# Scores in three parts, the last columns in two, and a new written-out order, in a sparse-attention and feed-forward kernel

## The chip, the cores and the metric

The kernel runs on one core of a Trainium2 chip. The metric is the device time of one execution in microseconds (us), the median over runs. Names of engines as the profile has them: PE is TensorE (matmuls; PEld is its weight load), ACT is ScalarE, DVE is VectorE, POOL is GpSimd and SP is SyncE. PEq, SPq, POOLq and ACTq are their instruction queues.

## What is computed

Sparse attention over 4 batches, 8 heads, 768 positions of 64 numbers: each query sees the keys less than 16 positions away, and one summary key (an elementwise maximum) and one mean value for each block of 32 positions. Its output, as 3072 rows of 512, goes through a feed-forward layer with a hard swish between two matrix products.

```python
k_sum = k.reshape(B, H, nb, block, D).max(axis=3)          # block = 32
v_sum = v.reshape(B, H, nb, block, D).mean(axis=3)
scores_l = scale * q @ k.T      # kept where |i - j| < 16
scores_s = scale * q @ k_sum.T + log(block)
a = softmax(concat(scores_l masked, scores_s))
x = a @ concat(v, v_sum)        # as [3072, 512]
h = x @ w_in                    # w_in [512, 2048]
g = h * clip(h + 3, 0, 6) / 6
out = g @ w_out                 # w_out [2048, 512]
```

## The kernel before

**Attention.** Queries go in tiles of 64 (12 a batch), each with a window of 96 keys and the 24 block keys, so 120 keys; a scores matmul gives keys down the partitions and queries along the columns. `kaug` holds windows and block maxima, `qT` the queries, `vaug` values with a column of ones (for the softmax sum) and the spread block sums, `at` the exponentials. Heads come in pairs p = 0 to 3. A batch is done in two halves of 384 queries; half 0 is tiles 6 to 11, half 1 tiles 0 to 5. Each half is one tile s of the feed-forward part (s = 0 to 7, 384 rows).

**Feed-forward.** `f1(s, ft)` (L656) makes 128 of the 2048 hidden columns: four matmuls of 384 columns, a relu on ACT (L670), and a gate on DVE (L671) that reads the same PSUM bank and the relu's result. For s = 0 and ft below 5 the four matmuls are operations of their own. `f2(s, ts, part)` (L674) sums 16 matmuls of 512 columns in four parts, then a copy to `ot` and a store by SP. For s = 7, ts = 1 the columns are done as two halves; the second half is copied as two quarters, one by ACT, which also issues its DMA (`finish`, L698), and one by DVE (L702), which SP stores (L703).

**PSUM.** Eight banks: three `h`, one `o`, and two `S` tiles of two banks. **The order.** Every operation is named: a letter, a place and a number (`s120.0` is the first operation of the scores of batch 1, heads u = 2, half 0). `ORDER` (L29) lists the names by hand as one sequence for all engines; `:A` or `:D` says which of ACT and DVE does an operation that either can do (`EITHER`). `Plan.issue` (L133) goes down the list, gives each buffer the slot of its pool that came free longest ago, and issues. Each engine then runs its own operations first in, first out, and waits by semaphores for what they read or overwrite; two engines' accesses to one PSUM tile are kept in list order as well. Tokens that begin with `~`, `-`, `_` or `=` are filler matmuls (`keep`, L778): n of 512, n of 128, n of 64 columns, or one of n x 64.

Letters: `c` constants (c.5 block indicator, c.6 and c.7 ones columns of `vaug`, c.8 to c.15 empty rows of `vaug`); `K Q V I O H` loads by POOL (`I` is w_in, `O` is w_out); `k` (L383) k transposes of batch 0, .1 block maxima, .2 and .3 copies of the halves, .4 the maxima's spread; `q` q transposes and copies (L410, L428); `h` copies of the neighbouring 32 rows of v (L357); `w` (L448) batches 1 to 3: transposes of k and q by DVE, neighbour rows, maxima, spread; `s` scores (L475, L501), with exponential on ACT and mask on DVE; `u` block sums of v and their copies (L526, L546); `v` values (L566, L609): matmuls, reciprocal and scale on DVE (L595), then for s below 4 a transpose on PE and a copy, else block transposes on DVE (L642) and four SP moves of four DMAs (L646); `F` and `G` are `f1` and `f2`. v03.5 is the last copy of batch 0's first half.

In `scores4` (L501) the scores of batches 1 to 3 are done for two head pairs u and one half: 48 matmuls of 64 columns into two `S` tiles, then for each tile an exponential of 120 x 768 (L520) and a mask of 96 x 768 (L521).

## Time and profile before

| | us |
|---|---|
| median of 3 runs | 217.43 |
| runs | 217.16 to 218.7 |
| span of the profiled execution | 215.4 |
| TensorE busy in it | 207.6 |
| VectorE busy in it | 162.1 |
| ScalarE busy in it | 136.0 |

The profiled execution has no time of its own beside its span (first to last instruction); the runs are timed from outside, some 2 us more. In the profile, a group's row has the line, engine, operation, output and inputs with shapes, the count, busy time and mean duration in ns, then the idle time of the engine ahead of them and what ended it. A row of the timeline has start, length, engine, line, what it does, how often, and in brackets the idle time ahead. A row by stage has the stretch, its length, then busy time and instructions of PE, PEld, DVE, ACT and POOL, the granted TensorE clock (1.00 is full), and the DMA engines' share and rate.

### The profile page before, as it was taken

How to read it: one execution, taken by the hardware profiler on the slowest of the kernel's cores; microseconds unless marked ns; L12 is line 12 of the kernel's file. 1: busy time of each engine (PE TensorE's matmuls, PEld its weight loads, DVE VectorE, ACT ScalarE, POOL GpSimd, SP SyncE). 2: the span in 40 equal slices, each digit the busy share in tenths (PEclk: the TensorE clock that was granted, in tenths of full speed). 3: DMA queues.
4: the chain of work that ended last, by engine and by line, in shares of the span. 5: the costliest groups of instructions: out<-in, count | busy, mean ns of one | idle time of the engine just before them, and what ended most of it. 6: DMA issues, size and time to landing. Idle time of an engine off the chain costs nothing.

```text
span 215.4 us, 6065 instructions
## 1 busy us (share of the span) xinstructions
PE 207.6 (96%) x2521; PEld 119.9 (56%) x2548; DVE 162.1 (75%) x318; ACT 136.0 (63%) x264; POOL 49.7 (23%) x66
## 2 busy tenths in 40 slices
...
DMA packets 91724, 22.68 MB, mean 105 GB/s; under 512 B 82224, under 2 KB 88752, under 8 KB 91696
## 3 DMA queue, kind: packets, MB, share of 16 engines
...
q8 instruction: 20, 0.33, 0.6%
q10 hardware_dynamic: 144, 0.07, 0.1%
q14 instruction: 8, 0.07, 0.1%
...
## 4 chain that ended last, share of the span: by engine, by line
PE 82%; SPq 5%; DMA 4%; issue 2%; DVE 2%; POOL 2%; ACT 1%; ACTq 0%; POOLq 0%
PE h L666 36%; PE o L683 29%; PE h L683 5%; SPq L648 4%; DMA first<-in_q_dram 3%; PE S L623 3%; PE S L512 2%; DMA out_dram<-ot 1%; ACT vaug L241 1%; POOL first L305 1%; PE S L636 1%; PE S L666 1%; PE h L581 1%; PE S L489 1%; PE S L553 1%
## 5 line engine op out<-in xcount | busy, mean ns | idle before, releaser
L666 PE MATMUL h<-x,win 128*128 128x384 bf16 x500 | 91.1, 326 | 0.1
L670 ACT ACTIVATE r<-h 128x384 f32<-128x384 f32 x125 | 58.7, 492 | 38.8 <-PE h L666 36.8
L671 DVE SCALAR_TENSOR_TENSOR g<-r,h 128x384 bf16<-128x384 f32 x125 | 65.9, 546 | 22.6 <-ACT r L670 20.0
L683 PE MATMUL o<-wout,g 128*128 128x512 bf16 x309 | 78.0, 379 | 1.9 <-issue 0.8
L666 PEld LDWEIGHTS <-win 128*128 128x128 bf16 x512 | 48.7, 98 | 35.5
L683 PEld LDWEIGHTS <-g 128*128 128x128 bf16 x400 | 38.4, 98 | 37.6 <-issue 0.3
L520 ACT ACTIVATE at<-S 120x768 bf16<-120x768 f32 x24 | 18.6, 810 | 5.5 <-PE S L512 5.4
L241 ACT COPY ot<-o 128x512 f32<-128x512 f32 x17 | 10.0, 587 | 15.4 <-PE o L683 14.2
L521 DVE TENSOR_TENSOR at<-at,mask 96x768 bf16<-96x768 bf16 x24 | 12.6, 549 | 2.0 <-ACT at L520 1.6
L605 DVE TENSOR_TENSOR xn<-S,rc 128x768 bf16<-128x768 f32 x14 | 13.3, 950 | 0.3
L343 POOL DMA_DIRECT2D vaug<-in_v_dram x10 | 11.9, 1194 | 0.4 <-DMA first<-in_k_dram 0.2
L241 DVE COPY ot<-h 128x512 f32<-128x512 f32 x2 | 1.3, 686 | 13.7 <-PE h L683 13.7
L683 PE MATMUL h<-wout,g 128*128 128x256 bf16 (+1 forms) x64 | 11.4, 326 | 0.0
L467 DVE TENSOR_REDUCE red<-kaug 128x24 bf16<-128x768 bf16 x12 | 11.2, 943 | 0.1
L241 ACT COPY vaug<-vaug 32x640 bf16<-32x640 bf16 (+3 forms) x17 | 8.9, 574 | 0.6 <-DMA vaug<-in_v_dram 0.3
L241 ACT COPY vaug<-vs 24x1536 bf16<-24x1536 bf16 x6 | 8.8, 1468 | 0.6 <-DVE vs L241 0.5
L782 PE MATMUL o<-idle 128*128 128x64 bf16 (+2 forms) x70 | 7.5, 287 | 1.1 <-DVE idle L287 1.1
L455 DVE STREAM_TRANSPOSE kaug<-kraw 128x768 bf16<-128x768 bf16 x8 | 8.1, 1025 | 0.3 <-PE S L512 0.3
L623 PEld LDWEIGHTS <-at 120*64 120x64 bf16 x336 | 6.3, 111 | 3.0 <-issue 1.6
L333 POOL DMA_DIRECT2D kraw<-in_k_dram x8 | 5.9, 740 | 8.5 <-DVE kaug L455 7.4
L642 DVE STREAM_TRANSPOSE y<-xn 128x768 bf16<-128x768 bf16 x8 | 7.6, 965 | 0.2
L512 PEld LDWEIGHTS <-kaug 32*128 32x128 bf16 x576 | 5.3, 92 | 4.4 <-issue 3.6
...
## 6 DMA issues: line engine op xcount, KB each, us to landing
out_dram<-ot SPq DMA_DIRECT2D x19, 256.0 KB, 2.3
vaug<-in_v_dram POOLq DMA_DIRECT2D x6, 384.0 KB, 12.9
...
win<-in_moe_w_in_dram POOLq DMA_DIRECT2D x3, 512.0 KB, 10.0
...
x<-y SPq DMA_DIRECT2D x64, 24.0 KB, 2.0
first<-in_k_dram POOLq DMA_DIRECT2D x6, 192.0 KB, 12.3
first<-in_q_dram POOLq DMA_DIRECT2D x6, 192.0 KB, 12.3
```

Source lines behind the costliest of these rows:

```text
L241: {"ACT": nc.scalar.copy, "DVE": nc.vector.tensor_copy, "POOL": nc.gpsimd.tensor_copy}[eng](o, i)
L343: op("POOL", "dma128", lambda: nc.gpsimd.dma_start(out=o[BLK:WIN, a:z, 0:D], in_=rows[:, a:z]), w=[("v", b % 2, c) for c in range(lo, hi)] ...
L467: op("DVE", "max", lambda: nc.vector.tensor_reduce(red.slot[:], w[:, :, BLK:WIN].rearrange("p t (n c) -> p t n c", n=2), axis=AX.X, op=ALU ...
L512: nc.tensor.matmul(X[g // 2].slot[:, g % 2, i * QB:(i + 1) * QB], kaug[2 * u + m][rows, t], qT[rows, 2 * u + m, t * QB:(t + 1) * QB], star ...
L520: op("ACT", "exp", lambda a=a, e=e: nc.scalar.activation(a, X[e].slot[0:KEYS, :, 0:HALF], AF.Exp, scale=scl), r=[X[e]], w=[("at", p, half)])
L521: op("DVE", "masking", lambda m=m: nc.vector.tensor_tensor(m, m, mask[:, low(half):low(half) + HQ].unsqueeze(1).to_broadcast([WIN, 2, HQ, ...
L605: nc.vector.tensor_tensor(o, src[..., 0:D], r.unsqueeze(len(r.shape)).to_broadcast(list(o.shape)), op=ALU.mult)
L623: nc.tensor.matmul(X.slot[64 * c:64 * c + 64, i, m:m + D + 1], a[:, t * QB:(t + 1) * QB], vaug[b % 2][0:KEYS, h, t, 0:D + 1], start=True, ...
L666: nc.tensor.matmul(bank(h)[:, 0:HALF], w_in_sb[:, kt, cols], xt[s].slot[:, kt], start=(kt == 0), stop=(kt == NP - 1))
L670: op("ACT", "relu", lambda: nc.scalar.activation(r.slot[:], bank(h)[:, 0:HALF], AF.Relu, bias=0.5, scale=1.0 / 6.0), r=[h], w=[r])
L671: op("DVE", "gate", lambda: nc.vector.scalar_tensor_tensor(gt[s].slot[:, ft], r.slot[:], 1.0, bank(h)[:, 0:HALF], op0=ALU.min, op1=ALU.mul ...
L683: nc.tensor.matmul(o.slot[:, a:z], gt[s].slot[:, ft, ts * 128:(ts + 1) * 128], w_out_sb[:, ft, a:z], start=(ft == 0), stop=(ft == NFT - 1))
```

## The change

Four things. `scores4` works in three parts of a batch in place of four: parts 0 and 1 are a pair u with tiles 4 to 11, part 2 is both pairs with tiles 0 to 3; each part is 64 matmuls, two exponentials of 120 x 1024, and masks (two of 96 x 1024, or four of 96 x 512). `at` becomes one tensor for that. The last tile's second half of columns becomes two groups of 16 matmuls of 128 columns: 384 to 512 ends as other tiles do (a copy, an SP store), 256 to 384 ends with ACT's copy and DMA. `ORDER` is rewritten from beginning to end, with other engines for some copies; it has no place where ACT and DVE read one PSUM tile next to each other. And the copy of q's first 16 columns has a key of its own (`qa`), for which only part 2 waits.

```diff
@@ -27,62 +27,62 @@
 ORDER = """
-c.0 K00.0 c.7 c.17 c.6 c.8:A K01.0 c.10:D c.5 c.1 _40 -15 k0.0 k0.2:A c.18 ~1 =2 k1.0 K02.0 ~12 =3 k2.0 k3.0 c.15:D c.2 c.3
-s000.0 k0.3:A c.13:D c.4 c.11:A k1.1 Q00.0 q0.0 k1.4 k0.1 c.20 k1.2:A Q01.0 ~2 =5 q1.0 k0.4 k1.3:D c.9:A c.14:A c.19 k2.3:A
-q0.1:A s000.1 q0.2:A =1 s010.0 s010.1 k2.2:A k3.2:D k3.3:D k3.1 V00.0 h000.0:D h001.0:D k2.1 k2.4 s000.2 ~2 =5 v00.0 V01.0 u0.0
-h010.0:D s020.0 c.16 s010.2 q1.2:A u0.3:D u0.1:D u0.4:D v01.0 v01.1 v01.2 v00.1 q1.1:A V02.0 h020.0:A h021.0:A h011.0:A v00.2
-s020.1 v01.3 v00.3 V03.0 u1.0 u1.3:A h030.0:D s030.0 k3.4 ~2 s030.1 u1.4:D v01.4 h031.0:D Q0w0.0 Q0w1.0 v01.5:D Q0w2.0 =1 q3.0
-q3.1:D q2.0 u1.1:A u1.2:D s020.2 v02.0 v02.1 v02.2 s021.0 v02.3 s030.2 v03.0 v03.1 q2.1:A v03.2 s011.0 v03.3 v00.4 v00.5:D v02.4
-s021.1 s011.1 s021.2 v03.4 v03.5:D s011.2 v02.5:A s031.0 s031.1 s001.0 s031.2 I2.0 F0x3.0 F0x3.1 F0x3.2 F0x3.3 F0x3.4 F0x3.5
-I4.0 F0x6.0 F0x6.1 F0x6.2 F0x4.0 F0x4.1 F0x4.2 F0x4.3 v411.0 v411.1 F0x5.0 F0x4.4 F0x4.5 v411.2 s001.1 I8.0 u0.2:A s001.2 F0x8.0
...
-G71x0.0 G62x0.4:D G62x0.5 F7x7.2 F7x11.0 F7x11.1 G61x0.0 F7x11.2 F7x14.0 G71x0.1 G71x0.2 G71x256.0 G61x0.1 F7x14.1 F7x14.2
-G71x0.3 G71x0.4:A G72x0.0 G72x0.1 G71x0.5 G41x0.5 G70x0.0 G61x0.2 G61x0.3 G61x0.4:A G52x0.5 G70x0.1 G70x0.2 G72x0.2 G50x0.0
-G50x0.1 G61x0.5 G50x0.2 G50x0.3 G72x0.3 G70x0.3 G50x0.4:A G50x0.5 G70x0.4:D G70x0.5 G60x0.0 G60x0.1 G60x0.2 G72x0.4:D G72x0.5
-G60x0.3 G71x256.1 G71x256.2 G60x0.4:D G60x0.5 G71x256.3 G71x256.4 G71x256.5 G71x256.6
+c.0 K00.0 K01.0 c.1 K02.0 _40 -14 k0.0 c.2 Q00.0 Q01.0 c.18 c.19 c.17 c.3 k0.1 =3 s010.0 =7 k1.0 k1.3:D c.16 s000.0 ~8 =6 k2.0
+c.6 k0.3:A k0.2:A k1.2:A k3.0 c.8:A V00.0 V01.0 c.20 c.4 k1.1 c.9:A k2.1 k3.3:A ~4 q0.0 k3.2:A c.5 k0.4 k2.4 k1.4 q0.1:A ~2 =3
+s000.1 k3.1 q0.2:A s000.2 =4 s010.1 s010.2 q1.0 V02.0 V03.0 h000.0:D q1.1:D k2.2:A =3 v00.0 s030.0 =7 s020.0 Q0w0.0 Q0w1.0
+k2.3:A u0.0 u0.1:A Q0w2.0 k3.4 q1.2:D c.10:D s030.1 s020.1 h010.0:D v01.0 u0.3:D I2.0 I4.0 h011.0:D I8.0 I0.0 I12.0 v01.1 v00.1
+s020.2 c.11:A s030.2 v01.2 h020.0:D v01.3 v00.2 v00.3 ~1 =6 v02.0 =6 v01.4 u0.2:D u1.0 u1.1:A v00.4 v01.5:D h030.0:D v00.5:A
+u1.3:A =5 v02.1 v03.0 v03.1 q3.0 v02.2 v02.3 v03.2 u0.4:D h001.0:A h031.0:A q3.1:D K13.0 q2.0 v02.4 v02.5:A =6 s031.0 q2.1:D
+v03.3 u1.2:D s031.1 K10.0 K12.0 F0x2.0 F0x3.0 F0x2.1 s001.0 v03.4 K11.0 Q1w1.0 s031.2 v03.5:D u1.4:D s001.1 s001.2 s011.0
+F0x3.1 F0x3.2 F0x2.2 F0x2.3 s011.1 s011.2 F0x3.3 s021.0 F0x3.4 F0x3.5 F0x2.4 s021.1 Q1w4.0 F0x5.0 F0x2.5 Q1w2.0 v410.0 v410.1
+F0x6.0 h021.0:A F0x7.0 F0x6.1 s021.2 v410.2 v411.0 F0x7.1 v410.3 v410.4:A F0x6.2 F0x7.2 v411.1 v411.2 F0x9.0 F0x9.1 F0x9.2
...
+V10.0 Q20.0 Q23.0 w12.0 w12.2 w12.3:D w12.1:D G02x0.3 G02x0.4:A K22.0 K21.0 Q22.0 K23.0 K20.0 V22.0 w13.3:D F1x12.2 c.15:D
+F1x4.2 s11.0 G00x0.0 G00x0.1 G00x0.2 G00x0.3 s11.1 s11.2 s10.4 c.13:D u4.0 h120.0:A s11.3 s11.4 h130.0:A G00x0.4:A h100.0:D
+h110.0:D s10.2 u4.1:A u4.4:A u4.3:D G01x0.0 u4.2:D h111.0:A G01x0.1 H2.0 v100.0 u4.5:D v101.0 v100.1 v101.1 v100.2 v101.2
...
+F4x13.2 w31.1 w30.2:A F4x6.1 w31.4:A F4x6.2 w32.1 F4x9.2 G32x0.3 w33.1 w32.2:A w33.3 F4x11.0 G22x0.5 v211.4 w33.4:D G32x0.4:A
+F4x11.1 u6.5:D F4x11.2 F4x7.0 v211.6 s30.0 F4x12.0 G30x0.0 G30x0.1 w32.5:A w32.4:A w31.5:D s30.3 s30.1 F4x7.1 F4x12.1 s31.0
...
+F4x3.0 F4x12.2 F4x3.1 G30x0.2 G30x0.3 s31.1 s31.3 v211.5 G20x0.5 F5x11.0 s30.4 F4x3.2 s30.2 F4x7.2 s31.4 G30x0.4:A F4x1.0
+F5x11.1 F5x7.0 F5x7.1 F4x1.1 w33.5:A s31.2 G32x0.5 F5x11.2 F5x7.2 w30.5:A v301.0 v300.0 v301.1 F4x1.2 v301.2 F4x5.0 F5x4.0
...
+G51x0.5 G71x0.2 F7x12.2 G70x0.0 G50x0.0 G71x0.3 G70x0.1 G50x0.1 G50x0.2 G50x0.3 G70x0.2 G71x0.4:D G50x0.4:A G60x0.0 G72x0.0
+G60x0.1 G60x0.2 G60x0.3 G72x0.1 G60x0.4:A G62x0.0 G62x0.1 G62x0.2 G62x0.3 G71x0.5 G50x0.5 G60x0.5 G62x0.4:A G62x0.5 G72x0.2
+G72x0.3 G61x0.0 G70x0.3 G61x0.1 G61x0.2 G61x0.3 G72x0.4:D G70x0.4:D G61x0.4:D G70x0.5 G72x0.5 G61x0.5 G71x384.0 G71x384.1
+G71x384.2 G71x384.3 G71x384.4:A G71x256.0 G71x256.1 G71x256.2 G71x256.3 G71x384.5 G71x256.4
@@ -183,6 +183,7 @@
     NS = S // 128
     LATE = 4
     SPLIT = 5
+    THIRD = NQ // 3
     EITHER = ("ACT", "DVE")
     ENGINE = {"DVE": nc.vector, "POOL": nc.gpsimd}
     ET = mybir.EngineType
@@ -200,7 +201,8 @@
     qT = sb([128, NP, PAD + S], BF16, "qT")
     first = sb([128, 2 * NP * NB, BLK], BF16, "first")
     kraw, qraw = ([sb([128, NP * NB, BLK], BF16, f"{n}raw"), first[:, i * NP * NB:(i + 1) * NP * NB]] for i, n in enumerate("kq"))
-    at = [sb([128, 2, S], BF16, f"at{p}") for p in range(NP)]
+    ats = sb([128, NP, 2, S], BF16, "at")
+    at = [ats[:, p] for p in range(NP)]
     vaug = [sb([128, H, NQ, VW], BF16, f"vaug{i}") for i in range(2)]
     knat, qnat = (first[0:RP].rearrange("p c x -> p (c x)")[:, lo:lo + H * n * D].rearrange("p (h s d) -> p h s d", h=H, s=n)
                   for lo, n in ((0, RUN), (H * RUN * D, RUN // 2)))
@@ -470,7 +472,10 @@
         op(EITHER, "maxspread", lambda eng: copy(eng, w[:, :, WIN:KEYS], red.slot[:].unsqueeze(1).to_broadcast([128, NQ, NB])),
            r=[red], w=[("km", p)])
         if b > 1:
-            op(EITHER, "around", lambda eng: copy(eng, qT[:, p, 0:PAD], qT[:, p, S:S + PAD]), r=[("q", p, 0)], w=[("q", p, 1)])
+            op(EITHER, "around", lambda eng: copy(eng, qT[:, p, 0:PAD], qT[:, p, S:S + PAD]), r=[("q", p, 0)], w=[("qa", p)])
+
+    def ats_of(p, half):
+        return [("at", p, x) for x in ((1, 2) if half else (0,))]
 
     def scores(b, p, half):
         plan.at(f"s{b}{p}{half}")
@@ -488,39 +493,47 @@
                     rows = slice(64 * j, 64 * j + 64)
                     nc.tensor.matmul(X.slot[:, j, i * QB:(i + 1) * QB], kaug[p][rows, t], qT[rows, p, t * QB:(t + 1) * QB],
                                      start=not masked, stop=not masked or i == HQ - 1)
-        op("PE", "scores", mms, r=[("ka", p, half), ("km", p), ("q", p, half)], w=[X], free=[("at", p, half)])
+        op("PE", "scores", mms, r=[("ka", p, half), ("km", p), ("q", p, half)], w=[X], free=ats_of(p, half))
         lo = low(half) * QB
         a = at[p][0:KEYS, :, lo:lo + HALF]
         m = at[p][0:WIN, :, lo:lo + HALF].rearrange("p j (t c) -> p j t c", c=QB)
-        op("ACT", "exp", lambda: nc.scalar.activation(a, X.slot[0:KEYS, :, 0:HALF], AF.Exp, scale=scl), r=[X], w=[("at", p, half)])
+        op("ACT", "exp", lambda: nc.scalar.activation(a, X.slot[0:KEYS, :, 0:HALF], AF.Exp, scale=scl), r=[X], w=ats_of(p, half))
         if not masked:
             op("DVE", "masking", lambda: nc.vector.tensor_tensor(
                 m, m, mask[:, low(half):low(half) + HQ].unsqueeze(1).to_broadcast([WIN, 2, HQ, QB]), op=ALU.mult),
-               r=["mask"], w=[("at", p, half)])
-
-    def scores4(b, u, half):
-
-        plan.at(f"s{b}{u}{half}")
+               r=["mask"], w=ats_of(p, half))
+
+    def scores4(b, part):
+
+        plan.at(f"s{b}{part}")
         X = [Buf("S"), Buf("S")]
+        us, ts = ((0, 1), (0, THIRD)) if part == 2 else ((part,), (THIRD, NQ))
+        n = (ts[1] - ts[0]) * QB
+        cols = slice(ts[0] * QB, ts[1] * QB)
 
         def mms():
-            for i in range(HQ):
-                t = low(half) + i
-                for m in range(2):
-                    for g in range(4):
-                        rows = slice(BLK * g, BLK * g + BLK)
-                        nc.tensor.matmul(X[g // 2].slot[:, g % 2, i * QB:(i + 1) * QB], kaug[2 * u + m][rows, t],
-                                         qT[rows, 2 * u + m, t * QB:(t + 1) * QB], start=m == 0, stop=m == 1)
-        ps_ = (2 * u, 2 * u + 1)
-        op("PE", "scores4", mms, r=[x for p in ps_ for x in (("ka", p, half), ("km", p), ("kh", p), ("q", p, half))], w=X, free=[("at", p, half) for p in ps_])
-        for e, p in enumerate(ps_):
-            lo = low(half) * QB
-            a = at[p][0:KEYS, :, lo:lo + HALF]
-            m = at[p][0:WIN, :, lo:lo + HALF].rearrange("p j (t c) -> p j t c", c=QB)
-            op("ACT", "exp", lambda a=a, e=e: nc.scalar.activation(a, X[e].slot[0:KEYS, :, 0:HALF], AF.Exp, scale=scl), r=[X[e]], w=[("at", p, half)])
-            op("DVE", "masking", lambda m=m: nc.vector.tensor_tensor(
-                m, m, mask[:, low(half):low(half) + HQ].unsqueeze(1).to_broadcast([WIN, 2, HQ, QB]), op=ALU.mult),
-               r=["mask"], w=[("at", p, half)])
+            for u in us:
+                for i, t in enumerate(range(*ts)):
+                    lo = us.index(u) * n + i * QB
+                    for m in range(2):
+                        for g in range(4):
+                            rows = slice(BLK * g, BLK * g + BLK)
+                            nc.tensor.matmul(X[g // 2].slot[:, g % 2, lo:lo + QB], kaug[2 * u + m][rows, t],
+                                             qT[rows, 2 * u + m, t * QB:(t + 1) * QB], start=m == 0, stop=m == 1)
+        ps_ = [2 * u + m for u in us for m in range(2)]
+        xs = (2,) if part == 2 else (0, 1)
+        op("PE", "scores4", mms, r=[x for p in ps_ for x in (("ka", p, 0), ("ka", p, 1), ("km", p), ("kh", p), ("q", p, 0), ("q", p, 1))]
+           + [("qa", p) for p in ps_ if part == 2 and b > 1], w=X, free=[("at", p, x) for p in ps_ for x in xs])
+        for e in range(2):
+            ps_ = [2 * u + e for u in us]
+            o = ats[0:KEYS, ps_[0]:ps_[-1] + 1:2, :, cols]
+            op("ACT", "exp1024", lambda o=o, e=e: nc.scalar.activation(o, X[e].slot[0:KEYS].rearrange("p j (u c) -> p u j c", c=n), AF.Exp, scale=scl),
+               r=[X[e]], w=[("at", p, x) for p in ps_ for x in xs])
+            for p in ps_:
+                m = at[p][0:WIN, :, cols].rearrange("p j (t c) -> p j t c", c=QB)
+                op("DVE", f"masking{n}", lambda m=m: nc.vector.tensor_tensor(
+                    m, m, mask[:, ts[0]:ts[1]].unsqueeze(1).to_broadcast([WIN, 2, ts[1] - ts[0], QB]), op=ALU.mult),
+                   r=["mask"], w=[("at", p, x) for x in xs])
 
 
     def vsum_first(g):
@@ -623,7 +636,7 @@
                             nc.tensor.matmul(X.slot[64 * c:64 * c + 64, i, m:m + D + 1], a[:, t * QB:(t + 1) * QB],
                                              vaug[b % 2][0:KEYS, h, t, 0:D + 1], start=True, stop=True)
         ps_ = (2 * g, 2 * g + 1)
-        op("PE", "values2", mms, r=[("at", p, half) for p in ((g, 2 + g) if b else ps_)] + [("v", b % 2, p) for p in ps_]
+        op("PE", "values2", mms, r=[x for p in ((g, 2 + g) if b else ps_) for x in ats_of(p, half)] + [("v", b % 2, p) for p in ps_]
            + [("vsum", b % 2, p) for p in ps_] + ([("vh", b % 2), ("vh0", b % 2)] if b > 1 else [("vh", b, p, half) for p in ps_]), w=[X])
         normal(X, rc, xn, 2, [("xn", s, g)], lambda: X.slot[:, :, 0:6 * (D + 1)].rearrange("p k (m c) -> p k m c", c=D + 1))
         xt.setdefault(s, Buf("x"))
@@ -692,16 +705,11 @@
                 if n:
                     nc.sync.dma_start(out=out[(b + 1) * S - n:(b + 1) * S, a:z], in_=ot.slot[0:n, a:z])
                 nc.sync.dma_start(out=out[b * S + row + n:b * S + row + 128, a:z], in_=ot.slot[n:128, a:z])
-            if a and n == 0:
-                m = (a + z) // 2
-
+            if z - a == d_model // 4 and z < d_model:
                 def finish():
-                    nc.scalar.copy(ot.slot[:, a:m], o.slot[:, a:m])
-                    nc.scalar.dma_start(out=out[b * S + row:b * S + row + 128, a:m], in_=ot.slot[:, a:m])
+                    nc.scalar.copy(ot.slot[:, a:z], o.slot[:, a:z])
+                    nc.scalar.dma_start(out=out[b * S + row:b * S + row + 128, a:z], in_=ot.slot[:, a:z])
                 op("ACT", "ofinish", finish, r=[o], touch=[ot])
-                op("DVE", "ocopy128", lambda: nc.vector.tensor_copy(ot.slot[:, m:z], o.slot[:, m:z]), r=[o], touch=[ot], w=["rest"])
-                op("SP", "store", lambda: nc.sync.dma_start(out=out[b * S + row:b * S + row + 128, m:z], in_=ot.slot[:, m:z]),
-                   r=["rest"], touch=[ot], size=z - m)
                 return
             op(EITHER, f"ocopy{z - a}", lambda eng: copy(eng, ot.slot[:, a:z], o.slot[:, a:z]), r=[o], w=[ot])
             op("SP", "store2" if n else "store", store, r=[ot], size=z - a)
@@ -755,9 +763,8 @@
         for half in range(2) if b == 1 else ():
             for g in range(2):
                 q_wide(b, half, g)
-        for half in range(2):
-            for u in range(2):
-                scores4(b, u, half)
+        for part in range(3):
+            scores4(b, part)
         vsum(b)
         for half in range(2):
             for g in range(2):
@@ -772,8 +779,8 @@
             if s < NTILE - 1 or i < 8:
                 f2(s, ts, part)
             else:
-                f2(s, ts, part, (0, d_model // 2))
-                f2(s, ts, part, (d_model // 2, d_model))
+                for a, z in ((0, 2), (2, 3), (3, 4)):
+                    f2(s, ts, part, (a * d_model // 4, z * d_model // 4))
 
     def keep(n, m, o):
         o = o[:, 0] if any(o is x for x in pairs) else o[:]
```

In the new order, between v03.5 and u4.5, there also stand c.7 (among the tiles F0x8 and F0x10), c.15 and c.13 (after F1x12 and around s11); in the old one all three stand ahead of v03.5.

80 lines of the change are left out of this document (36 added, 44 removed).

## The prediction

> **What bounds the kernel now.** I read the page first: busy times, chain, groups. Then the busy time of each engine by stage, and who waited for whom on TensorE after the first stage.
>
> ```profile
> span 215.4 us, 6065 instructions
> PE 207.6 (96%) x2521; PEld 119.9 (56%) x2548; DVE 162.1 (75%) x318; ACT 136.0 (63%) x264; POOL 49.7 (23%) x66
> ```
>
> ```profile
> 4.85:24.60 19.75, 18.75 (x397) 12.13 (x396) 16.70 (x50) 16.17 (x32) 15.56 (x20) 1.00 1.71 173
> 24.60:54.00 29.40, 28.85 (x391) 17.18 (x393) 27.33 (x53) 23.68 (x47) 16.21 (x20) 1.00 1.76 184
> ```
>
> ```profile
> PE o L683 <- issue: 0.8, 5, 0.2
> PE S L623 <- issue: 0.3, 1, 0.3
> ```
>
> TensorE is busy in 96% of the span, and after 24.6 us its listed waits come to 1.1 us in all. A busy TensorE need not be at its peak, so I look at the pitch, from start to start, in long runs of one shape.
>
> ```profile
> 33.98 1.46 PE L666 MATMUL h<-x,win 128*128 128x384 bf16 x8
> ...
> 35.28 0.98 PE L666 MATMUL S<-x,win 128*128 128x384 bf16 x5
> ```
>
> ```profile
> 207.21 3.62 PE L683 MATMUL o<-wout,g 128*128 128x512 bf16 x16
> 210.67 1.47 PE L683 MATMUL h<-wout,g 128*128 128x256 bf16 x12
> 212.22 0.27 ACT L699 COPY ot<-h 128x128 f32<-128x128 f32 x1 [5.90 <-PE h L683]
> 212.52 0.37 ACTq L700 DMA_DIRECT2D out_dram<-ot  x1
> 212.52 0.29 DVE L702 COPY ot<-h 128x128 f32<-128x128 f32 x1 [0.90 <-ACT ot L699]
> 212.84 0.33 SPq L703 DMA_DIRECT2D out_dram<-ot  x1
> ```
>
> Eight 384-column matmuls go from 33.98 to the next start at 35.28: 0.16 us each. Sixteen of 512 columns go from 207.21 to 210.67: 0.216 each. The feed-forward part is 512 of the first and 384 of the second (32 of these cut in half): about 83 + 83 us that no order changes. So the time is three sums: when TensorE first has enough to do, what it then has left with its stalls, and what follows its last matmul (210.67 + 1.47 = 212.14, to 215.44).
>
> The first of these is no TensorE time. Its 18.75 busy of 19.75 us hold filler on the idle tile.
>
> ```profile
> 5.43 7.02 DMA first<-in_q_dram
> ...
> 23.05 0.57 DVE xn L605
> 23.66 0.34 PE h L589 x3
> 24.00 0.46 PE S L489 x24
> ```
>
> ```profile
> 4.85 0.26 DVE L261 TENSOR_SCALAR bias<-band 96x384 bf16<-96x384 bf16 x1 [0.26 <-POOL band L257]
> ...
> 5.87 1.31 ACT L241 COPY kaug<-h 128x576 bf16<-128x576 bf16 x4 [2.93 <-PE h L391]
> ...
> 13.43 1.00 DVE L241 COPY vaug<-vaug 32x768 bf16<-32x768 bf16 x3 [0.44 <-DMA vaug<-in_v_dram]
> ```
>
> ```profile
> 24.25 0.35 DVE L241 COPY x<-h 128x384 bf16<-128x384 bf16 x1
> 24.39 2.12 PE L666 MATMUL h<-x,win 128*128 128x384 bf16 x12
> 29.49 1.48 DVE L671 SCALAR_TENSOR_TENSOR g<-r,h 128x384 bf16<-128x384 f32 x3
> 30.16 0.57 PE L623 MATMUL S<-vaug,at 120*64 120x65 bf16 x24
> ```
>
> The chain of waits goes from the second q load (landed at 12.45) through scores, exponentials, normalisation and transposes of the first half of batch 0 to the first F matmul at 24.39. The copy that completes its input, v03.5, is the VectorE row that starts at 24.25 and ends at 24.60. VectorE is busy 16.70 of the 19.75 us before that, the fullest engine there with real work.
>
> **The start.** The POOL queue issues the same loads in the same order up to and including the fourth output weight (its DMA comes after those that the start needs), so landings don't move: zero, from the order itself. Fillers are equal too (19x512 + 15x128 + 40x64 + 17x64 columns before, 15x512 + 14x128 + 40x64 + 56x64 after: 15616 against 15296).
>
> ```profile
> L282 DVE MEMSET vaug<- 32x768 f32 x3 | 2.1, 698 | 0.4 <-issue 0.2
> L241 DVE COPY vaug<-vaug 32x768 bf16<-32x768 bf16 x5 | 1.8, 359 | 1.9 <-PE S L553 0.8 <-PE o L535 0.6 <-DMA vaug<-in_v_dram 0.4
> L241 DVE COPY kaug<-h 128x480 bf16<-128x480 bf16 x1 | 0.7, 651 | 0.0
> L241 DVE COPY x<-h 128x384 bf16<-128x384 bf16 x2 | 0.7, 344 | 0.0
> ```
>
> VectorE's work between 4.85 and v03.5 changes by instructions that change engine or side. Out go c.13 (0.70), k3.2 and k3.3 (0.65 and some 0.75 for the one like it with two edge pieces), four copies of the halo and spread kind (h001, h031, u0.1, u1.4: 0.36 to 0.45 each), v00.5 (0.34) and one mask (0.55): about 4.6. In come q1.1 and q1.2 (0.34 each), q2.1 (some 0.5: twice the columns of v00.5), h011, h020 and u0.2 (some 0.4 each), one mask (0.55), and c.5, c.6 and c.10, which before stood ahead of 4.85 in time that VectorE had free (0.70 for c.10, I take 1.1 for the other two, fills of short pieces): 4.8. Back-to-back instructions overlap by some 0.07 (three gates in 1.48, not 1.64), the same for both. Net: zero, within 0.3.
>
> What can shrink is the 3.05 us of VectorE idling. After the change it waits for the first k transposes (from 4.85 + 0.26 = 5.11 to 5.87, where the trace has their first reader), for V at 13.43 (0.4), and some 0.6 for the block sums of v; with 0.8 of small gaps as now that is 2.6. The second pair of exponentials follows the first sooner, since three halo copies no longer stand ahead of it on ScalarE, so the last normalisation finds its values ready. So v03.5 ends at 24.60 - 0.45, say 24.2; bounds 23.7 (gaps as short as the 0.4) and 24.8 (idle as before, plus the 0.2 of one more late copy).
>
> TensorE gets ahead meanwhile: six F matmuls (kt = 0 to 2 of two tiles) run before v03.4's copy is out: 6 x 0.16 = 0.98. s021 is still owed (12 matmuls; 24 take 0.46 in the chain above, so 0.25). Net 0.7 less to do from 24.25 on than before from 24.39.
>
> **From there on.** Scores of batches 1 to 3: 192 matmuls a batch before and after: zero on TensorE.
>
> ```profile
> L670 ACT ACTIVATE r<-h 128x384 f32<-128x384 f32 x125 | 58.7, 492 | 38.8 <-PE h L666 36.8
> L671 DVE SCALAR_TENSOR_TENSOR g<-r,h 128x384 bf16<-128x384 f32 x125 | 65.9, 546 | 22.6 <-ACT r L670 20.0
> L520 ACT ACTIVATE at<-S 120x768 bf16<-120x768 f32 x24 | 18.6, 810 | 5.5 <-PE S L512 5.4
> L521 DVE TENSOR_TENSOR at<-at,mask 96x768 bf16<-96x768 bf16 x24 | 12.6, 549 | 2.0 <-ACT at L520 1.6
> ...
> L605 DVE TENSOR_TENSOR xn<-S,rc 128x768 bf16<-128x768 f32 x14 | 13.3, 950 | 0.3
> ...
> L455 DVE STREAM_TRANSPOSE kaug<-kraw 128x768 bf16<-128x768 bf16 x8 | 8.1, 1025 | 0.3 <-PE S L512 0.3
> ```
>
> Eight exponentials of 768 become six of 1024. From 384 to 768 elements is 492 to 810, so 0.83 ns an element, and 1024 is about 1.02: 6.1 against 6.5 a batch, 1.1 us less ScalarE in all. ScalarE idles 38.8 us for F alone: covered, zero. Masks: the same number and elements, zero.
>
> VectorE is the cover that thins. c.7, c.13 and c.15 (0.5, 0.7 and 0.7), a spread (u1.4) and a wider q copy now come after v03.5. I add its queue up, at durations less 0.07, from v03.5 to u4.5 (the last copy that v101 waits for): 31 gates 14.8, 7 masks 4.1, 4 turns with their 4 maxima 7.3 (these priced a little under the turns), two normalisations 2.3, fills 1.9, copies 4.9: 35.3 us. TensorE's work to the same place, by the pitches, is 34.6, and its real pace is 1.017 of such a sum (187.75 from 24.39 to 212.14, for 184.6): 35.2. Before, the same two are 32.9 and 36.1. Close by, at F0x9, which waits for the gate F0x6.2 to free its bank: 4.4 on VectorE (three gates, three masks, a normalisation, a copy) against 3.9 (two single F matmuls, three F, s021, two groups of 24 at 0.5, a transpose). So VectorE goes from 3.2 us in hand to none: TensorE will wait for it. I take 0.5; bounds 0 (its pace is what it needs) and 2 (it keeps the 93% of 27.33 in 29.40, so 35.3 takes 38.0). Behind a gate that is late stand the next F matmul and all that follows on TensorE.
>
> SyncE moves too: stores are issued elsewhere, and one store buffer is held to near the end.
>
> ```profile
> 100.03 10.68 SPq L648 DMA_DIRECT2D x<-y  x16
> ```
>
> ```profile
> out_dram<-ot SPq DMA_DIRECT2D x19, 256.0 KB, 2.3
> ...
> x<-y SPq DMA_DIRECT2D x64, 24.0 KB, 2.0
> ```
>
> Half a batch of moves takes 10.7 us of issue and 2.0 to land. Counted from v03.5, batch 2's second half of moves can start near 89 us (VectorE's sum to its last block transposition). G22's store stands one move (2.7) behind, out near 92 and landed (2.3 for a store) near 94.5; G32's copy, which takes its buffer, comes near 95.6 by TensorE's sum. The last move lands near 89 + 10.7 + 0.5 + 2.0 = 102.2, and F5 starts near 102.4. I take zero, bounds 0 and 1.5. Behind the G32 copy on ScalarE stand the relus of F4, behind F5 all of TensorE.
>
> **The tail.** Before: ScalarE copies 128 columns (0.27), then VectorE the others of the same bank (0.29), then SyncE issues. VectorE's row says it waited for ScalarE. After: the 128 columns to 512 end 0.9 us earlier (16 matmuls at 0.056, estimated from a quarter of 0.216), and only ScalarE's copy and its DMA follow the last matmul.
>
> ```profile
> out_dram<-ot ACTq DMA_DIRECT2D x1, 64.0 KB, 1.7
> out_dram<-ot SPq DMA_DIRECT2D x1, 64.0 KB, 1.6
> ```
>
> Before: 212.84 + 1.6 = 214.4 landed, 1.0 before the end. After: 0.08 + 0.27 + 0.03 + 1.7 + 1.0 = 3.1 from the last matmul in place of 3.3: 0.2 gained. Bounds: 0 and 0.3 (a copy of 0.29 gone). The 32 narrow matmuls in place of 16 wide ones cost 0.05.
>
> The row shows that the two reads of one bank went one after the other. [...]
>
> **Sum.** TensorE's last matmul: 212.14 - 0.14 (24.25 for 24.39) - 0.7 + 0.05 + 0.5 = 211.85; plus 3.1 = 214.95, against 215.44: 0.5 us less. The profiled span is 2.0 under the median of the runs (217.43), so I predict 216.9.
>
> **The rivals.** Slower: VectorE becomes the bound. For it speaks that its sum reaches TensorE's up to u4.5; against it, that the 93% it was busy was not forced, since TensorE waited for nothing. If it holds 93% and no more, 38.0 - 35.2 = 2.8 us are lost by v101, and I put half as much again on the later batches, where its sum stays within 1 us of TensorE's: 217.4 - 1.0 + 4.2 = 220.6 (1.0 is the forecast's gain without the 0.5). It decides from 95% on (35.3 / 0.95 = 37.2): 2.0 lost, more than the 1.0 gained. Second: SyncE is late, and G32's copy and F5 hold TensorE for 1.5 us: 218.4. Third: the start packs better, v03.5 at 23.7, no wait for VectorE, and the 1.1 us of listed waits go: 216.9 - 0.5 - 0.5 - 1.1 = 214.8. Fourth: nothing that it moves was on the path, 217.4.
>
> **Chances.** Forecast 0.44, VectorE 0.25, SyncE 0.10, better start 0.13, nothing 0.08. This kernel's measurement tells about 1% (2.2 us) from no change. Faster by more than that: 0.13, the third rival. Within: forecast, nothing, and SyncE's greater part: 0.60. Slower: VectorE and the rest: 0.27. The range reaches down to 215.1 (the better start, in part) and up to 219.6 (most of VectorE's).
>
> **What would show it.** v03.5 ending near 24.2 shows the start; F matmuls ahead of it show the 0.7. Waits of TensorE's F for VectorE's gate between 28 and 62 us show the thin cover; over 1.5 us of them make the forecast wrong, as does a wait of ScalarE for an output DMA near 120 us. VectorE idle before 4.85 in place of its fills shows where they went. In the tail, only ScalarE's copy after the last matmul.

## The result, and the profile after

| | before | after |
|---|---|---|
| median | 217.66 us (4 runs) | 223.92 us (4 runs) |
| runs | 217.16 to 218.7 | 222.46 to 224.69 |
| profiled execution: span | 215.4 | 220.7 |

The ratio is 1.027 (95% interval 1.022 to 1.032): the changed kernel is slower. I had forecast 216.9 and a range of 215.1 to 219.6.

The page of the changed kernel, its first lines:

```profile
span 220.7 us, 6126 instructions
...
PE 210.2 (95%) x2564; PEld 120.3 (55%) x2564; DVE 159.4 (72%) x310; ACT 133.2 (60%) x266; POOL 49.3 (22%) x66
```

VectorE and ScalarE have less to do than before (162.1 and 136.0). TensorE is listed as 2.6 us busier (207.6 before), but its work is the same to 0.2 us: the fillers have 320 columns more (0.13 at 0.216 us for 512) and the narrow matmuls of the tail cost 0.05 (32 at 0.056 us in place of 16 at 0.109). In the profile before, 27 matmul records are missing (x2521, with x2548 weight loads); a profile of nearly the same kernel without that fault (e4) has 208.6, and the rest of the difference was not traced. So the 5.3 us are lost time, most of it waits. Who TensorE waited for after 24.6 us (engine, tile and line, for whom: us in total, times, longest):

```profile
PE o L696 <- ACT ot L243: 3.1, 1, 3.1
PE h L679 <- DMA x<-y: 1.2, 2, 0.7
PE S L636 <- DVE vaug L243: 0.3, 1, 0.3
PE S L521 <- DVE qT L461: 0.2, 1, 0.2
PE h L679 <- issue: 0.2, 1, 0.2
```

One wait is most of it. The timeline of TensorE and ScalarE around it (G00 is the 16 matmuls at 54.59, G01 starts at 62.12):

```profile
54.59 3.61 PE L696 MATMUL o<-wout,g 128*128 128x512 bf16 x16
54.61 1.02 ACT L530 ACTIVATE at<-S 120x1024 bf16<-120x1024 f32 x1
...
58.13 0.85 PE L566 MATMUL S<-vaug,ind 96*32 96x128 bf16 x48
...
59.13 0.83 ACT L243 COPY vaug<-vaug 32x768 bf16<-32x768 bf16 x1 [3.49 <-PE S L566]
59.86 1.01 ACT L530 ACTIVATE at<-S 120x1024 bf16<-120x1024 f32 x1
60.78 0.81 ACT L243 COPY vaug<-vaug 32x768 bf16<-32x768 bf16 x1
...
61.50 0.57 ACT L243 COPY ot<-o 128x512 f32<-128x512 f32 x1
...
62.12 1.89 PE L696 MATMUL o<-wout,g 128*128 128x512 bf16 x8 [3.13 <-ACT ot L243]
```

Read it from the bottom. G01 needs the only `o` bank, and the copy of G00 out of it (61.50) is what it waits for. G00 had been done at 58.2. In ScalarE's queue three things stand ahead of that copy: a halo copy of v (h120), an exponential (s11.3), a halo copy (h130). The first of them idled ScalarE for 3.49 us, waiting for the block sums u4.0 (58.13), since these read the rows that it overwrites; and u4.0 stands on TensorE behind all of G00. So TensorE waits for ScalarE, which waited for TensorE. In the order before, G00x0.4 stood ahead of u4.0 and of h120. There the copy starts 0.1 us after u4.0, while u4.0 runs, and G01 follows u4.0 with no wait:

```profile
56.09 1.67 PE L683 MATMUL o<-wout,g 128*128 128x512 bf16 x7 [0.16 <-issue]
...
57.70 0.85 PE L553 MATMUL S<-vaug,ind 96*32 96x128 bf16 x48
...
57.81 0.59 ACT L241 COPY ot<-o 128x512 f32<-128x512 f32 x1 [0.30 <-PE o L683]
...
58.48 2.76 PE L683 MATMUL o<-wout,g 128*128 128x512 bf16 x11
58.60 0.83 ACT L241 COPY vaug<-vaug 32x768 bf16<-32x768 bf16 x1 [0.20 <-PE S L553]
```

To place the rest I take the time at which an instruction of TensorE starts, less the sum of all work issued to TensorE until then at the pitches of its shapes. This lost time grows by, in us:

| stretch (us) | before | after | what TensorE waits for there, after |
|---|---|---|---|
| 0 to 57 | 14.2 | 13.9 | start and inputs |
| 57 to 64 | 0.1 | 3.3 | the copy G00x0.4 |
| 64 to 70 | 0.1 | 0.7 | spreads of the block sums, a scale, both VectorE |
| 70 to 115 | 0.7 | 0.8 | |
| 115 to 122 | 0.0 | 0.8 | SyncE's moves, at F4x0.0 |
| 122 to 172 | 0.5 | 0.9 | |
| 172 to the last matmul | 0.1 | 0.8 | SyncE's moves, at F7x2.0 |
| last matmul to the end | 3.3 | 3.0 | |

The column after sums to 5.2 more than the column before, which is the 5.3 of the spans within the rounding. The median has risen by about 1 us more than the span; e3 and e6 show what is behind that.

SyncE's queue, where the last of the moves for F7 stand behind two stores:

```profile
105.04 17.14 SPq L661 DMA_DIRECT2D x<-y  x20
...
168.83 0.54 SPq L706 DMA_DIRECT2D out_dram<-ot  x1
169.41 0.42 SPq L707 DMA_DIRECT2D out_dram<-ot  x1
169.87 2.59 SPq L661 DMA_DIRECT2D x<-y  x4
```

The start, by VectorE's timeline and by two stretches (length, then busy PE, PEld, DVE, ACT, POOL):

```profile
4.86 0.26 DVE L263 TENSOR_SCALAR bias<-band 96x384 bf16<-96x384 bf16 x1 [3.61 <-POOL band L259]
...
22.51 1.02 DVE L243 COPY qT<-S 128x768 bf16<-128x768 bf16 x2
...
25.02 0.34 DVE L243 COPY x<-o 128x384 bf16<-128x384 bf16 x1
```

```profile
4.85:24.60 19.75, 18.53 (x378) 12.11 (x379) 16.78 (x48) 14.94 (x33) 15.54 (x20) 1.00 1.71 174
4.85:25.38 20.53, 19.31 (x389) 12.60 (x389) 17.54 (x49) 15.72 (x34) 15.54 (x20) 1.00 1.69 175
```

v03.5 is the copy at 25.02; it ends at 25.36, not at 24.2. And the tail:

```profile
215.80 1.95 PE L696 MATMUL h<-wout,g 128*128 128x128 bf16 x32
...
216.94 0.27 ACT L243 COPY ot<-h 128x128 f32<-128x128 f32 x1 [6.35 <-PE h L696]
217.79 0.27 ACT L710 COPY ot<-h 128x128 f32<-128x128 f32 x1 [0.58 <-PE h L696]
218.08 0.37 ACTq L711 DMA_DIRECT2D out_dram<-ot  x1
```

### The profile page after: what moved, and what is told of

The parts are those of the page before. It is cut to its first block, busy times and chain, and to the rows that moved or that the text cites. A ratio compares the mean times of both kernels' runs of the same rounds, so it can differ in the third digit from the quotient of the medians.

```text
span 220.7 us, 6126 instructions
## 1 busy us (share of the span) xinstructions
PE 210.2 (95%) x2564; PEld 120.3 (55%) x2564; DVE 159.4 (72%) x310; ACT 133.2 (60%) x266; POOL 49.3 (22%) x66
## 4 chain that ended last, share of the span: by engine, by line
PE 78%; DVE 8%; SPq 6%; issue 3%; ACT 2%; DMA 2%; DVEq 0%
PE h L679 32%; PE o L696 27%; SPq L661 5%; PE h L696 5%; PE o L789 3%; PE S L521 2%; PE S L636 2%; DVE vaug L243 2%; DVE g L684 2%; DMA x<-y 2%; DVE qT L461 1%; PE S L566 1%; PE h L393 1%; PE S L649 1%; PE h L548 1%
## 5 line engine op out<-in xcount | busy, mean ns | idle before, releaser
L696 PE MATMUL o<-wout,g 128*128 128x512 bf16 x336 | 81.0, 379 | 3.2 <-ACT ot L243 3.1
L684 DVE SCALAR_TENSOR_TENSOR g<-r,h 128x384 bf16<-128x384 f32 x125 | 65.2, 544 | 25.3 <-ACT r L683 24.1
L696 PEld LDWEIGHTS <-g 128*128 128x128 bf16 x416 | 39.2, 98 | 41.9 <-issue 3.1
L243 ACT COPY ot<-o 128x512 f32<-128x512 f32 x19 | 11.2, 588 | 21.6 <-PE o L696 21.5
L530 ACT ACTIVATE at<-S 120x1024 bf16<-120x1024 f32 x18 | 17.9, 1023 | 1.7 <-PE S L521 1.5
L534 DVE TENSOR_TENSOR at<-at,mask 96x1024 bf16<-96x1024 bf16 (+1 forms) x24 | 12.5, 545 | 4.3 <-ACT at L530 4.2
L243 DVE COPY ot<-h 128x512 f32<-128x512 f32 (+1 forms) x3 | 1.8, 603 | 16.4 <-PE h L696 16.4
L618 DVE TENSOR_TENSOR xn<-S,rc 128x768 bf16<-128x768 f32 x14 | 13.1, 944 | 0.1
L696 PE MATMUL h<-wout,g 128*128 128x512 bf16 (+2 forms) x80 | 12.1, 294 | 0.0
L789 PE MATMUL o<-idle 128*128 128x64 bf16 (+4 forms) x66 | 6.8, 278 | 1.1 <-DVE idle L289 1.1
L789 PEld LDWEIGHTS <-idle 128*128 128x128 bf16 x80 | 5.8, 123 | 3.0 <-DVE idle L289 1.1
```

Of the source, the lines that this page charges most:

```text
L243: {"ACT": nc.scalar.copy, "DVE": nc.vector.tensor_copy, "POOL": nc.gpsimd.tensor_copy}[eng](o, i)
L530: op("ACT", "exp1024", lambda o=o, e=e: nc.scalar.activation(o, X[e].slot[0:KEYS].rearrange("p j (u c) -> p u j c", c=n), AF.Exp, scale=sc ...
L534: op("DVE", f"masking{n}", lambda m=m: nc.vector.tensor_tensor(m, m, mask[:, ts[0]:ts[1]].unsqueeze(1).to_broadcast([WIN, 2, ts[1] - ts[0] ...
L618: nc.vector.tensor_tensor(o, src[..., 0:D], r.unsqueeze(len(r.shape)).to_broadcast(list(o.shape)), op=ALU.mult)
L684: op("DVE", "gate", lambda: nc.vector.scalar_tensor_tensor(gt[s].slot[:, ft], r.slot[:], 1.0, bank(h)[:, 0:HALF], op0=ALU.min, op1=ALU.mul ...
L696: nc.tensor.matmul(o.slot[:, a:z], gt[s].slot[:, ft, ts * 128:(ts + 1) * 128], w_out_sb[:, ft, a:z], start=(ft == 0), stop=(ft == NFT - 1))
```

## The experiments

Theory A: the wait at 62 is an accident of ScalarE's queue. B: VectorE is late, as my first rival had it, and the waits are its. C: SyncE's moves are late by their place. D (formed on the way): TensorE's clock. All kernels but e4, e7 and e8 are the changed kernel with the edit shown in `ORDER` (dots and notes in round brackets mark what is left out here); nothing of the computation is left out in any.

**e1: the copy first**

```diff
-s10.4 c.13:D u4.0 h120.0:A s11.3 s11.4 h130.0:A G00x0.4:A
+s10.4 s11.3 G00x0.4:A c.13:D u4.0 h120.0:A s11.4 h130.0:A
```

> The changed kernel with two of ScalarE's operations moved ahead of the halo copy: the exponential s11.3, then the copy G00x0.4 that frees the only o bank, then the halo copies h120 and h130. Theory A (ScalarE's queue: h120 waits for the block sums u4.0, which on TensorE stand behind all of G00, and behind h120 waits the copy for which TensorE holds G01): TensorE's wait of 3.13 us before G01x0.0 at 62.12 goes, G01x0.0 starts near 59.0; the halo copies now come last, so up to 1 us may come back at v100 or v101. Profiled span 220.7 - 3.1 to 220.7 - 2.1, so 217.6 to 218.6. Theory B (VectorE's work is the cover that became the bound, the wait for the copy only stands in its place): TensorE waits for VectorE in the same stretch, span above 220.0. Theory C (SyncE's moves are late and cost most): above 220.0 as well.

Span 218.0, median 219.66 (before: 217.17), ratio 1.013 (1.007 to 1.019). TensorE's waits after 24.6:

```profile
PE S L636 <- DVE vaug L243: 1.6, 1, 1.6
PE S L521 <- DVE qT L461: 0.2, 1, 0.2
```

The 3.1 are gone, 1.6 came back one step further (v100, for halo copies and spreads that now come last), and the waits for moves went as well. A holds.

**e2: the sums sooner**

```diff
-s11.0 G00x0.0 G00x0.1 G00x0.2 G00x0.3 s11.1 s11.2 s10.4 c.13:D u4.0 h120.0:A
+c.13:D s11.0 s11.1 G00x0.0 u4.0 G00x0.1 G00x0.2 G00x0.3 s11.2 s10.4 h120.0:A
```

> The changed kernel with ScalarE's queue as it was, but what h120 waits for comes sooner: the block sums u4.0 stand on TensorE behind the first quarter of G00 in place of behind all of it, with the fill c.13 and the exponential s11.1 ahead of them. Theory A: u4.0 runs from about 55.7 to 56.6, h120 from 56.7, then s11.3, h130 and the copy as before, 3.2 us in all, so the copy ends near 59.9 while G00 ends near 59.1: of the 3.1 us of waiting some 0.8 stays. Span near 218.4 (217.8 to 219.2). If it is the place of the copy as such and not the wait for the sums, the wait stays as long as it was: 220.7. Theory B: above 220.0.

Span 218.8, median 220.67, ratio 1.015 (1.010 to 1.020). The wait for the copy is 0.7. ScalarE's queue is untouched here; only what its head waits for came sooner, so it is that wait, not the copy's place alone. The waits for moves stay (1.2), and v100 waits 0.8 where it waited 0.3.

**e3: the moves sooner**

```diff
-v200.2 F3x14.0 G22x0.1 H3.0 F3x6.2 F3x13.2 F3x2.0 F3x11.0 G22x0.2 w21.5:A G22x0.3 v201.2 v200.3 v201.3
+v200.2 v201.2 v200.3 v201.3 F3x14.0 G22x0.1 H3.0 G22x0.2 G22x0.3 F3x6.2 F3x13.2 F3x2.0 F3x11.0 w21.5:A
-G30x0.5 ... v311.7
+v311.7 G30x0.5
```

> The changed kernel with ScalarE's queue as it was, and two things taken out of the way of SyncE's moves: the block transposition v201.3 and what leads to it stand ahead of two gates on VectorE (and two quarters of G22 ahead of two F on TensorE as cover), which lets the 16 moves for tile 4 start about 1.2 us sooner than 104.97; and the store G30x0.5 stands behind the last move v311.7 for tile 7 instead of ahead of it, about 1 us. Theory C: TensorE's waits for moves at F4x0.0 (0.85) and F7x2.0 (0.67) go, span 220.7 - 1.5 = 219.2; with theory A alone, they are real but small, so at most these 1.5 go and the 3.13 stay: 219.2 to 219.8. If moves were hidden anyway, 220.7. If the two gates that now come later hold TensorE, some of the 1.5 comes back there.

Span 220.8, median 222.91: a miss by the total. The waits for moves at F4x0.0 and F7x2.0 did go (lost time from 70 us on grows by 2.2 against 3.1), so C is real, 0.9 net with 0.35 given back to a gate, for the F matmul at 105.2. What hid it is in the timeline behind the wait, first of e3, and in the stretch 62 to 65, of e3 and then of the changed kernel (the figure behind POOL is the granted clock):

```profile
61.98 3.48 PE L696 MATMUL o<-wout,g 128*128 128x512 bf16 x8 [3.13 <-ACT ot L243]
```

```profile
62.00:65.00 3.00, 3.00 (x8) 1.00 (x7) 2.84 (x6) 2.94 (x5) 1.71 (x2) 0.50 2.45 159
```

```profile
62.00:65.00 3.00, 2.55 (x49) 1.44 (x50) 2.84 (x7) 2.94 (x6) 1.66 (x2) 1.00 2.45 159
```

The same eight matmuls behind the same wait take 3.48 us at a granted clock of 0.50, 1.89 at 1.00. So in e3 the low clock behind the wait costs another 1.6 us.

**e4: the wait made in the kernel before**

```diff
-G00x0.4:A V12.0 u4.0 h130.0:D h120.0:A F1x0.1
+V12.0 u4.0 h130.0:D h120.0:A G00x0.4:A F1x0.1
```

> The kernel before with one operation moved: G00x0.4 (the copy that frees the o bank) stands on ScalarE behind the halo copy h120 in place of ahead of the block sums. Here u4.0 follows G00x0.3 on TensorE at once, so the wait is short. Theory A: TensorE's G01x0.0, at 58.48 before, waits for h120 (58.60 to 59.43) and the copy (0.59): it starts near 60.1, 1.5 us more, and nothing later gives that back, since TensorE has hardly a wait left: span 215.4 + 1.5 = 216.9 (216.4 to 217.2). If TensorE's time there is not what sets the end (theory B in that VectorE has the longer path), 215.4 to 215.8.

Median 218.24 against 217.17, ratio 1.005 (1.003 to 1.008); span 216.2.

```profile
PE o L684 <- ACT ot L242: 1.4, 1, 1.4
```

The wait is there with its forecast size and is not given back: lost time grows by 1.6 from 57 to 64. The span shows 0.8 of it because this execution had lost 0.5 to 0.8 less by 57; starts differ by that much between executions. The intervals hold 0.6 to 1.6 us.

**e5: the stretch in another order**

```diff
-s11.0 G00x0.0 G00x0.1 G00x0.2 G00x0.3 s11.1 s11.2 s10.4 c.13:D u4.0 h120.0:A s11.3 s11.4 h130.0:A G00x0.4:A h100.0:D h110.0:D s10.2 u4.1:A u4.4:A
+c.13:D s11.0 s11.1 s11.3 G00x0.0 G00x0.1 s11.2 s10.4 u4.0 u4.1:A u4.4:A h120.0:D h130.0:D h100.0:D h110.0:D G00x0.2 G00x0.3 s11.4 G00x0.4:A s10.2
```

> The changed kernel with the stretch from 54 to 62 us put in another order: block sums u4.0 behind the second quarter of G00 (the fill c.13 and the exponentials s11.1 and s11.3 ahead of them), the sums' cast and first spread directly behind on ScalarE, the halo copies h120 and h130 on VectorE (0.35 us there, 0.83 on ScalarE), and then the copy G00x0.4. Theory A: the wait of 3.13 before G01x0.0 and the one at v100 go without a new one; TensorE ends 3.3 + 0.5 sooner, span near 216.8 if the waits for SyncE's moves at F4x0.0 and F7x2.0 (0.85 and 0.67) stay. Theory C1 (these two waits are no cause of their own, but follow from VectorE being late since the stretch at 62): they go too, as they did with the copy moved first, span near 215.4. Start-up differs by up to 0.5 between executions. Theory B (VectorE's sum is the bound): above 218.

Span 217.7, median 220.06, ratio 1.012. The 3.1 shrank to 0.7, as in e2, where G01 follows G00 with nothing between too, and 0.5 is at v100. Of the moves' waits 0.3 is left at F4x0.0 and none at F7x2.0; a gate's wait of 0.5 is new at 131. Neither 216.8 nor 215.4: the waits for moves are partly C1's, and others come.

**e6: the wait filled**

```diff
-G01x0.0
+~13 G01x0.0
```

> The changed kernel with 13 filler matmuls of 512 columns on the idle tile (13 x 0.216 = 2.8 us) just ahead of G01x0.0, in the time that TensorE waits there anyway; nothing else is changed, and no result uses them. Theory D (after the wait of 3.1 us TensorE is granted half its clock for some 3 us in most executions, as the execution with the moves early showed: granted clock 0.50 from 62 to 65 us): the wait stays, the granted clock is 0.997 or more in all runs, the profiled span stays 220.7 (220.3 to 221.3), and the median falls from 223.9 to 222.4, some 1.5 less. If the low clock of 0.984 in three of four runs has another cause, it stays in about as many runs and the median stays near 223.9.

```profile
59.89 2.98 PE L789 MATMUL h<-idle 128*128 128x512 bf16 x13
63.08 1.89 PE L696 MATMUL o<-wout,g 128*128 128x512 bf16 x7 [0.22 <-ACT ot L243]
```

The wait is the same, now with TensorE busy in it, and the clock behind it is full (1.00 from 62 to 65 us). Median 221.86 (ratio 1.019, 1.016 to 1.022) in place of 223.92, the spans of its four runs 219.8 to 220.6 in place of 220.7 to 223.0: 2 us, a little more than the 1.5 expected. A mean clock of 0.990 and 0.992 in two of the runs missed my 0.997; in the profiled one the low clock lies elsewhere, in the start, with a mean of 0.66 from 20 to 25 us:

```profile
20.00:25.00 5.00, 4.15 (x62) 3.07 (x61) 3.33 (x8) 2.99 (x7) 2.47 (x4) 0.66 1.26 206
```

**e7: the tail alone, in the kernel before**

```diff
-... G71x256.0 ... G71x256.1 G71x256.2 ... G71x256.3 G71x256.4 G71x256.5 G71x256.6
+... G71x384.0 ... G71x384.1 G71x384.2 ... G71x384.3 G71x384.4:A G71x256.0 G71x256.1 G71x256.2 G71x256.3 G71x384.5 G71x256.4
```

with the change's own edit of `f2` and of its loop.

> The kernel before with the change's last part alone: the last half of the columns in two groups of 128, the last one ending with ScalarE's copy and DMA. TensorE's last matmul to the end is 3.30 us before and 2.99 in the changed kernel. If the part does by itself what the traces show, the span is 0.3 less, and the median 216.9 against 217.2, ratio 0.9986. If the 16 narrow matmuls more cost as much as the tail gains: ratio 1.000.

Median 217.03 (12 runs) against 217.45, ratio 0.998 (0.996 to 0.999), span 215.2, last matmul to end 3.0. The part does by itself what the trace shows. This is the one kernel here that is faster than both, by 0.2% of the kernel before.

**e8: three parts alone, in the old order**

```diff
(operations as a whole, without their numbers)
-s100 ... s101 ... s110 ... w21.0 w20.0 w21.3 w21.2:A ... s111     (four parts)
+s10  ...          s11  ... s12.0 w21.0 w20.0 w21.3 w21.2:A s12.1   (three; so for batches 2 and 3)
```

> The kernel before with the scores of batches 1 to 3 in three parts, in the old order as far as it allows: parts 0 and 1 in the places of the first half's scores, part 2 in that of the second half's, and the four operations that turn batch 2's first keys behind batch 1's part 2. If the form of the scores is worth nothing (the same matmuls, 1.1 us less ScalarE that had idle time) and the loss is the order's, the span is 215.4 and the median 217.2, each within 0.6. If the larger exponentials and the wait for both halves' inputs hold the values up, TensorE waits at v100 to v301 for at or masks, and the span is 216.5 or more.

Span 219.7, median 220.92, ratio 1.017 (1.013 to 1.020). First who TensorE waits for, then VectorE at 67:

```profile
PE h L679 <- DVE g L684: 2.1, 2, 1.7
...
PE S L521 <- ACT x L243: 0.8, 1, 0.8
PE S L521 <- ACT qT L243: 0.3, 1, 0.3
```

```profile
67.10 1.92 DVE L457 STREAM_TRANSPOSE kaug<-first 128x768 bf16<-128x768 bf16 x2 [1.72 <-PE S L521]
```

Part 2 reads the keys of all pairs, so the turns of the next batch's keys, which overwrite them, wait for it on VectorE, and a gate behind them holds TensorE 1.7 us. That is my placing of part 2, not the cost of an exponential. It was the only placing tried, so whether the three parts could be had in the old order for nothing isn't shown. In the changed order the stretch with batch 2's scores (70 to 115 us) loses hardly more than before, 0.8 against 0.7.

**e9, e10, e11: halo copies ahead of the sums; with the moves of e3; with the old start**

```diff
-s10.4 c.13:D u4.0 h120.0:A s11.3 s11.4 h130.0:A G00x0.4:A h100.0:D h110.0:D s10.2
+s10.4 h120.0:D h130.0:D h100.0:D h110.0:D s11.3 G00x0.4:A u4.0 s11.4 s10.2        (c.13:D ahead of s11.0)
```

This is e9; e10 has the edit of e3 as well, and e11 also the list of the kernel before up to s031.2, ahead of the first F matmul.

> The changed kernel with the four halo copies of batch 1 ahead of the block sums u4.0 in the order, as the kernel before has two of them, all on VectorE (0.35 us each), and the copy G00x0.4 directly behind the exponential s11.3; the fill c.13 comes sooner for that. Then no copy waits for the sums, and u4.0 itself (0.85) is the cover between G00 and G01. Theory A: no wait over 0.3 us of TensorE from 54 to 66 us; lost time there 0.5 instead of 4.2, span 220.7 - 3.7 = 217.0 with the waits for moves as they were (1.5), 215.8 with the part of them gone that goes when VectorE is not late, as in the runs with the copy first and with the stretch mended. Theory B (VectorE's sum is the bound of this stretch): TensorE waits for VectorE's gates or spreads for over 1 us between 56 and 75 us.

> The kernel of the run with the halo copies ahead of the sums, and with it the earlier block transposition v201.3 and the store G30x0.5 behind the last move. Theory C: what waits for moves are left there (0.3 to 1.2 us) go, and 0.3 come as a gate's wait near 102 us: span 0.2 to 0.9 less than without. Near 215.6. If the moves only cost where VectorE was late, no difference (within the 0.5 of the starts).

> The kernel of the run with halo copies and moves mended, with the order of the kernel before up to the first F matmul in front, and the rest of the changed order behind it (its 0.8 us later v03.5 goes: in four executions of old starts v03.5 ended at 24.60, 24.48, 24.35 and 25.16, in six of new ones at 25.36, 25.94, 25.01, 25.23, 25.10 and 26.13). If the time at which v03.5 ends is what TensorE's end hangs on, 0.8 less: 214.8. If the F matmuls that the new order runs ahead of it pay for that, as the lost time at 30 us says (13.3 us against 13.1 on average), 0.2 less: 215.4.

Spans 218.9, 218.6 and 217.8; medians 220.01, 219.79 and 219.32 against 216.82; ratios 1.015, 1.012 and 1.010. No wait for the copy is left, but u4.0 now waits 1.2 us for VectorE in e9, which needed 2.85 us for the four halo copies, not 4 x 0.35:

```profile
57.14 2.85 DVE L243 COPY vaug<-vaug 32x768 bf16<-32x768 bf16 x4
```

What the same copy took in other places stands in the last section.

The medians of e9, e10 and e11 differ by 0.2 to 0.7 and their intervals overlap, so no gain is shown by e10 or e11. In the profile of e10 the waits for moves are gone (1.0 in e9), but 0.7 for gates came. In e11 v03.5 ends at 25.0 in place of 26.4 in e10, and the lost time by 30 us is 0.4 less.

**e12, e13: the fills back into VectorE's free time; with it, halo copies ahead of the sums, two on each engine**

```diff
-c.17 c.3
+c.17 c.6 c.7 c.10:D c.5 c.15:D c.13:D c.3
 (these six taken out of their later places; e13 also:)
-u4.0 h120.0:A s11.3 s11.4 h130.0:A G00x0.4:A h100.0:D h110.0:D s10.2
+h120.0:A s11.3 h110.0:A h130.0:D h100.0:D G00x0.4:A u4.0 s11.4 s10.2
```

> The changed kernel with six fills on VectorE (c.5, c.6, c.7, c.10, c.13, c.15; 3.4 us) back in the time before 4.86 us in which VectorE waits 3.61 for the band; nothing else is moved. Theory B (beside the wait of 3.1, VectorE's work is late and what it delays costs TensorE 1.5 to 2 us): v03.5 ends near 24.3 in place of 25.4 (1.6 of fills less ahead of it, part of that idle), the waits at v100 and for the moves at F4x0.0 and F7x2.0 shrink or go, the wait before G01x0.0 stays near 3.1; span 220.7 - 0.7 (start) - 0.5 (v100) - 0.9 (moves) = 218.6, 218 to 219.5. If these fills are hidden as they are, 220.7 (220.2 to 221.2).

> The six fills in VectorE's free time before 4.86 us, and with it the halo copies ahead of the block sums, two on ScalarE and two on VectorE, and G00x0.4 directly behind them. Theories A and B together hold for all that the order lost: no wait over 0.4 us of TensorE after 24.6 but 0.5 for a move, span 215.4 - 0.3 (tail) to 216.2. If something else is left, span 217 or more, as the mended kernels so far (217.7 to 218.9).

VectorE's busy time from 25 to 58 us: before, after, and in e12.

```profile
25.00:58.00 33.00, 32.29 (x473) 18.85 (x478) 30.68 (x60) 26.93 (x52) 19.20 (x22) 1.00 1.77 185
```

```profile
25.00:58.00 33.00, 32.86 (x453) 19.02 (x451) 31.59 (x62) 25.89 (x53) 18.18 (x21) 1.00 1.78 183
```

```profile
25.00:58.00 33.00, 32.78 (x478) 19.21 (x480) 29.34 (x56) 25.27 (x52) 18.14 (x22) 1.00 1.77 184
```

Who TensorE waits for in e12, then in e13:

```profile
PE o L696 <- ACT ot L243: 3.1, 1, 3.1
PE h L679 <- DMA x<-y: 0.9, 2, 0.7
PE S L521 <- DVE qT L461: 0.2, 1, 0.2
```

```profile
PE S L636 <- DVE vaug L243: 0.9, 1, 0.9
PE h L679 <- DMA x<-y: 0.4, 1, 0.4
PE S L521 <- DVE qT L461: 0.2, 1, 0.2
PE h L679 <- issue: 0.2, 1, 0.2
```

In e12 VectorE is less busy (29.34 us of the 33, against 31.59), v03.5 ends at 24.63, and lost time at 57 is 13.4 in place of 13.9. The waits for moves stay at 0.9, and so does the 3.1. By the span nothing is gained (220.6; median 223.09): in this execution the clock is low behind the wait (0.79 from 58 to 66), and lost time from 57 to 70 grows by 5.1, in the changed kernel by 4.0. The wait at v100 is gone, but that isn't the fills' doing for certain: it is gone in e3 too, where the fills are as they were and the clock is low in the same place (0.50 from 62 to 65), so that TensorE comes later to v100 (at 65.39, in the changed kernel at 64.34). And the sooner start didn't come again: in e13, with the same fills, v03.5 ends at 25.64, and lost time at 57 is 0.5 more than in the changed kernel. So what B is worth isn't shown; the moves' waits are not its doing alone.

e13 has span 217.8 and median 218.62 (8 runs, 216.3 to 217.8 by span), ratio 1.006 (1.002 to 1.009): the nearest that the changed order comes to the old. By what I expected, a span of 217 or more says that something else is left; five of the eight lie under 217, all of them over the 216.2 that I gave for A and B together. It still waits 0.9 at v100 and 0.4 for moves.

## Why the prediction was wrong

The step that failed is one sentence: "ScalarE idles 38.8 us for F alone: covered, zero." Total idle time says that ScalarE has room. It doesn't say that an operation at the head of its queue isn't waiting for TensorE while TensorE needs the one behind it. I did ask what is queued behind what for G32's copy and for the gates; I didn't go through ScalarE's part of the new list, where h120 stands ahead of G00x0.4 and u4.0 behind G00x0.3. Shown cost: a wait of 3.1 us in the profiled execution (gone or shrunk in e1, e2, e5, e9, e13, each by another edit; a shorter one made in the old kernel by e4). The clock behind it adds 1.6 in e3's profile, and filling the wait takes 2 off the median (e6). None of my rivals had it. The VectorE rival's 220.6 was a median, 3.3 under the measured 223.92; that the profiled span is 220.7 is no support for it, and its mechanism is another. Neither of the two signs that I had named as making the forecast wrong came: F waited for gates by 0.26 in all from 28 to 62 us, not 1.5, and ScalarE waited for no output DMA near 120.

By the other steps:

- *The start*, forecast v03.5 at 24.2 and 0.85 less for TensorE. It ends at 25.0 to 26.4 in the eight executions that were profiled with the new start, at 24.3 to 25.2 in the five with the old. "Net: zero" was mis-sized: VectorE was busy 17.54 us up to v03.5 where it had been 16.70, and idled 2.99, not 2.6. The six F matmuls ahead of the end of v03.4's copy came as forecast, three from 23.40 and three from 24.83, and pay for it: lost time at 30 us is 13.2 against 13.1. So 0.1 more in place of 0.85 less.
- *VectorE's thin cover*, 0.5 with bounds 0 and 2. The direction was right: VectorE is 96% busy from 25 to 58 us in place of 93%. That is also past the 95% at which I let the rival decide: VectorE can be filled further than the rival had it. F waits for a gate once, by 0.26 ahead of the matmul at 39.35, and TensorE waits 0.3 at v100; both together are near the forecast 0.5. There is no chain of late gates. The 3.61 us in which VectorE idles before 4.86 are where the fills had been, as told.
- *SyncE*, taken at zero with a bound of 1.5. The listed waits come to 1.2, at F4x0.0 and F7x2.0, and by lost time the two stretches hold 1.5 more than before; e3 took out 0.9 net. The bound was just reached, and zero was too low, since I had looked at G32's copy and at F5, which wait for nothing; the moves of tile 4 and the stores ahead of v311.7 I had not gone through.
- *The tail*, 0.2 forecast, 0.3 measured, twice (2.99 and 3.0 for 3.3), with the working as written: only ScalarE's copy follows. Whether the two reads of one bank could have run at the same time before was not tried.
- *The third rival's 1.1 us of listed waits* were no waits. In rows of the kernel before that end by "issue", start to start is 432 ns, twice 216: a matmul's record is missing there. In the profile of e4, where no record is missing, no such row stands. TensorE of the kernel before had next to nothing to give.
- *Two slips in the working*: the sums of filler columns are exchanged (15296 before, 15616 after), and beside the upper bound of 2 for VectorE the same sum gives 38.0 - 35.2 = 2.8. Neither bears on the result.

Still open: with the copy, the halo copies and the fills mended (e13), lost time is 1.1 more from 57 to 64 and 0.9 more from 100 to 172 us than before. Which of the many moved operations hold it was not taken apart, and of the start only that it varies by more than its parts are worth.
